# Gate sums moved from the v passes to VectorE beside the products, weights' pieces in one stream through the change of halves, last rows on another queue

## The chip, the cores and the metric

One core of one Trainium2 chip runs the whole program in one launch. The metric is device microseconds of that core; lower is better. The program is one long list of instructions for five engines (TensorE or PE, VectorE or DVE, ScalarE or ACT, GpSimd or POOL, SyncE or SP), each of which works through its own list strictly in order and waits on semaphores. SP does nothing but issue transfers; GpSimd computes and issues some.

## The reference

Input x has 2048 tokens of 1024 values. A is linear attention with 32 heads of 32, B is softmax attention with 32 heads of 32, each with its own qkv weights (1024 by 3072) and output weights (1024 by 1024). A gate mixes them per token:

```python
x = A_x
g = _sigmoid((x * gate_w).sum(-1, keepdims=True))
a = _A_ref(x, A_wqkv, A_wo)
b = _B_ref(x, B_wqkv, B_wo)
return g * a + (1 - g) * b
```

## The kernel before, in words

Every product of two fp32 matrices is done as three matmuls (`three`, from line 148): each operand is split into a high part (a cast on ScalarE, line 293) and a low part (a subtraction on VectorE, line 294), and high-high, high-low and low-high are added up in a PSUM bank of 128 by 512. A 128x512 matmul is the unit.

The work has two parts. The first, up to about 480 us, is written out by hand: for each half J of the tokens (J = 0, 1; 1024 tokens, two column blocks jj) come **v passes** and then **quads**. The second, from there to the end, is a list planned at build time (`linear`, `maxima`, `heads_`, `output`), with a model of each engine's time in `T`.

**v passes** (`v_pass`, line 427, with the loops of both halves that call it). For k = 0 to 7, one 128-row block of x and of B's v weights: x is loaded, split, and 8 banks get 24 matmuls. Raw blocks stay in four raw tiles per pair of k, from which `sides` (four VectorE differences) and `split_sides` make the operands T1, T2 and T3 of a Strassen-like product. At the end the 8 banks are copied by ScalarE to SBUF (`v_out`, line 357) through four buffers, `v_outs`, and stored. After that TensorE can use the banks again.

**Quads** (`quad`, line 475; `quads`, line 631). Eight per half; one quad makes two column blocks of q or k in seven products of 12 matmuls each, on six banks in turn. ScalarE and VectorE combine the products (lines 495 to 514), split the results and SP stores them (`qk<-mid`). After each product (and what is emitted behind it) `next(side)` advances side streams by one **turn**; `beside` advances several. Turns are an order in the program, not a time: an engine gets to what a turn emitted when it has done all before it. The streams are the next quad's weights (`quad_weights`), T4's split (`late_side`), the spill of x to DRAM (`spill_rest`), the gate, and the pieces of B's output weights.

**Ring.** Weights of v passes and quads lie in a ring of 13 pairs of places (`RINGW`), used in turn.

**Gate.** `gate_add` (line 383) runs inside the v passes: for each k and jj ScalarE multiplies a raw x block by the gate weights of its rows (line 388) into a scratch tile of the quads (P1, C11, H11, W2), and GpSimd adds that into `gate_sum` (line 390). During the quads eight one-column matmuls sum over the rows, and ScalarE takes the exponential.

**Pieces** (`wo_parts`, from line 522). B's output weights in 4 row pieces of 7 combinations: ScalarE casts the high part (532), GpSimd subtracts the low part (533), may form the next difference (line 550 and the like) and load the next raw piece (529), and stores both parts to DRAM (537). One pair of buffers serves all pieces, so a cast waits for the stores before. A piece is issued every `PIECE_STEP` = 3 turns, 14 pieces in each half's quads; none in a half's last quad or in the v passes.

**Tail.** When the last softmax head is done (`finish`, `store_part`, line 1300), its 32 rows are copied from SBUF into the output stage's operand tiles (`load_rest`, line 1607, its transfer 1611), four token blocks at a time, by SP. SP's list at this place also holds whole weight tensors of 1 MB (`big<-woS`, `big<-woW`) and the linear branch's rows (`big<-ra`). The output stage's first full product, X21, needs the rows; line 1680 adds a product onto the linear branch's rows.

Of the kernel before, what the change touches and what calls it, by code (L numbers as in the profile page):

```python
# [41 lines left out]
PIECE_STEP = 3  # L42
# [6 lines left out]
def kernel(  # L49
# [73 lines left out]
    big = [None if i in (15, 18, 20) else big_tile(i, F32R) for i in range(NBIG)]  # L123
# [218 lines left out]
    RAW_BIG = (20, 15, 18)  # L342
# [8 lines left out]
    v_outs = [P1, C11, H11, W2]  # L351
# [11 lines left out]
    gate_wt, gate_sum, gate_b = kvb[:, 0, :NK], halves(zrep), bank[6]  # L363

    def gate(J):

        yield
        yield
        for t in range(2 * TPC):
            nc.tensor.matmul(gate_b[:, t:t + 1], gate_sum[t // TPC][:, t % TPC * P:(t % TPC + 1) * P], ones[:, :1],  # L370
                             start=True, stop=True)
        g = g_sb[:, 2 * TPC * J:2 * TPC * (J + 1)]
        nc.scalar.activation(g, gate_b[:, :2 * TPC], AF.Exp, scale=-1.0)
        yield
        if J:
            nc.vector.tensor_scalar_add(g_sb, g_sb, 1.0)
            nc.vector.reciprocal(g_sb, g_sb)
            nc.vector.tensor_scalar(omg_sb, g_sb, -1.0, 1.0, op0=ALU.mult, op1=ALU.add)
            yield

    gate_t = [C11, H11, P1, W2]

    def gate_add(raws, k):

        for jj in range(2):
            acc, raw, w = gate_sum[jj], raws[jj + 2 * (k % 2)], gate_wt[:, k:k + 1]
            to = gate_t[(2 * k + jj) % len(gate_t)] if k else acc
            nc.scalar.activation(to, raw, AF.Copy, scale=w)
            if k:
                nc.gpsimd.tensor_add(acc, acc, to)  # L390
# [57 lines left out]
    def quad_weights(raws, J, f):  # L448
# [7 lines left out]
        part(0, w11)  # L456
        part(6, w22)
# [10 lines left out]
        yield  # L468
# [53 lines left out]
    def wo_parts(i0, i1):  # L522

        z0, z1 = halves(zrep)
        hi_w, lo_w = (big[15][:, i * C:(i + 1) * C] for i in (2, 3))

        def load(z, m, i, **add):
            if i < i1:
# [17 lines left out]
        for _ in range(PIECE_STEP):  # L546
            yield
# [1352 lines left out]
```

## Time and profile before

| | |
|---|---|
| median of 3 runs | 2876.86 us (2874.42 to 2880.17) |
| the profiled execution's own time | 2881.64 us |
| its span, first to last instruction | 2879.9 us |
| TensorE busy | 98% |
| VectorE, GpSimd, ScalarE busy | 82%, 72%, 57% |
| mean granted TensorE clock | 0.990 |
| HBM over the span | 151 GB/s |

Busy shares are means over the whole span; the stages before 480 us and the tail behind 2700 us differ from it. A full stretch of 20 us holds 90 matmuls of 128x512.

### The profile page before, as it was taken

The numbers are of one execution on the slowest core, as the hardware profiler recorded it, in microseconds if no ns is written. First come the engines' busy times: TensorE is split into PE (matmuls) and PEld (weight loads), VectorE is DVE, ScalarE is ACT, GpSimd is POOL, SyncE is SP. The second block draws the span as 40 slices with busy tenths as digits, with TensorE's granted clock in tenths as the row PEclk, the third lists the DMA queues.
The fourth block names the chain that finished last, engine by engine and source line by source line (L and its number), as shares of the span: only waits on it lengthen the run. The fifth ranks groups of instructions, "written<-read, shape, count | busy, mean of one in ns | idle before, by whom it ended". The sixth has DMA issues, their size and how long they took to land.

```text
span 2879.9 us, 46927 instructions
## 1 busy us (share of the span) xinstructions
PE 2815.7 (98%) x15880; PEld 2051.5 (71%) x15880; DVE 2348.8 (82%) x3745; ACT 1649.3 (57%) x3093; POOL 2073.2 (72%) x1078
## 2 busy tenths in 40 slices
PE   8998999999999999999999999999999999999899
PEld 6876777777667766776677767776776667666587
DVE  7877774788888888888888888888878888887678
ACT  5334432176666666666676666666666566656422
POOL 3333234099999999999899999889879988887000
PEclk9999999999999999999999999999999999999999
DMA  7886888633343334343433344455666555545764
GB/s 231 260 260 193 258 272 236 204 96 99 99 123 95 102 105 132 97 105 99 115 104 101 104 116 138 149 170 178 180 189 182 143 155 142 144 119 158 259 198 154
DMA packets 398988, 451.14 MB, mean 157 GB/s; under 512 B 106382, under 2 KB 234638, under 8 KB 396956
## 3 DMA queue, kind: packets, MB, share of 16 engines
q1 hardware_dynamic: 377244, 410.90, 47.1%
q0 software_dynamic: 21504, 37.24, 6.0%
q8 instruction: 127, 2.08, 0.3%
q14 instruction: 113, 0.93, 0.1%
HBM read 305.93 MB, written 127.66 MB: 151 GB/s over the span
## 4 chain that ended last, share of the span: by engine, by line
PE 80%; DMA 3%; DVE 1%; issue 1%; SPq 1%; ACT 0%; POOL 0%; ACTq 0%; DVEq 0%; POOLq 0%
PE bank L1358 16%; PE bank L1216 16%; PE bank L1508 15%; PE bank L152 10%; PE bank L155 10%; PE bank L157 10%; DMA woS<-big 1%; DMA v<-mid 1%; PE bank L1280 1%; SPq L169 1%; PE bank L1006 0%; PE bank L895 0%; DMA xh<-mid 0%; DMA xh<-xs 0%; DVE big L294 0%
## 5 line engine op out<-in xcount | busy, mean ns | idle before, releaser
L1443 POOL TENSOR_TENSOR big<-big,big 128x512 f32<-128x512 f32 (+2 forms) x694 | 1641.7, 2370 | 108.2 <-ACT big L1361 65.3
L1221 DVE TENSOR_REDUCE mx<-bank 128x1 f32<-128x512 f32 x2048 | 1313.5, 683 | 303.3 <-PE bank L1216 299.9
L1361 ACT ACTIVATE big<-bank 128x512 f32<-128x512 f32 x2048 | 1179.8, 602 | 432.9 <-PE bank L1358 368.2
L1358 PE MATMUL bank<-big,big 128*128 128x512 f32 x1888 | 742.1, 394 | 1.7 <-DMA big<-ml 1.2
L1216 PE MATMUL bank<-big,big 128*128 128x512 f32 x1888 | 739.8, 392 | 1.3 <-ACT big L1361 1.3
L152 PE MATMUL bank<-big,big 128*128 128x512 f32 x1576 | 622.2, 395 | 43.6 <-ACT mid L357 17.4
L157 PE MATMUL bank<-big,big 128*128 128x512 f32 x1572 | 618.5, 393 | 4.7 <-DVE big L294 4.6
L155 PE MATMUL bank<-big,big 128*128 128x512 f32 x1576 | 619.2, 393 | 1.6 <-DVE big L294 1.4
L1508 PE MATMUL bank<-big,mid 128*32 128x512 f32 x4096 | 454.2, 593 | 0.0
L1358 PEld LDWEIGHTS bank<-big,big 128*128 128x128 f32 x1888 | 354.3, 188 | 126.8 <-issue 47.8
L1216 PEld LDWEIGHTS bank<-big,big 128*128 128x128 f32 x1888 | 354.9, 188 | 75.2 <-ACT big L1361 2.6
L152 PEld LDWEIGHTS bank<-big,big 128*128 128x128 f32 x1576 | 299.1, 190 | 112.5 <-ACT mid L357 18.2
L157 PEld LDWEIGHTS bank<-big,big 128*128 128x128 f32 x1572 | 297.9, 190 | 72.3 <-DVE big L294 9.0
L155 PEld LDWEIGHTS bank<-big,big 128*128 128x128 f32 x1576 | 299.4, 190 | 65.5 <-DVE big L294 2.9
L1508 PEld LDWEIGHTS bank<-big,mid 128*32 128x32 f32 x4096 | 143.9, 110 | 264.1 <-issue 263.8
L1459 DVE TENSOR_TENSOR bank<-bank,big 128x512 f32<-128x512 f32 x364 | 251.7, 691 | 5.3 <-ACT big L1361 3.0
L294 DVE TENSOR_TENSOR big<-mid,big 128x512 fp32r<-128x512 f32 (+1 forms) x157 | 119.5, 777 | 61.2 <-ACT big L293 61.1
L533 POOL TENSOR_TENSOR big<-zrep,big 128x512 fp32r<-128x512 f32 x28 | 37.2, 1330 | 171.6 <-ACT big L532 94.1
L1439 POOL TENSOR_TENSOR big<-big,big 128x1536 f32<-128x1536 f32 (+1 forms) x31 | 123.3, 3977 | 44.4 <-ACT big L1361 44.2
L293 ACT CAST big<-mid 128x512 fp32r<-128x512 f32 (+1 forms) x157 | 92.5, 616 | 108.0 <-DVE mid L1627 66.7
L152 PE MATMUL bank<-big,xh 128*128 128x512 f32 x376 | 148.5, 395 | 5.4 <-DMA xh<-xs 5.4
L155 PE MATMUL bank<-big,xh 128*128 128x512 f32 x376 | 148.1, 394 | 0.0
(156 smaller groups left out, 2234.5 us busy)
## 6 DMA issues: line engine op xcount, KB each, us to landing
big<-xs SPq DMA_DIRECT2D x288, 256.0 KB
big<-qk SPq DMA_DIRECT2D x690, 64.0 KB
xh<-xs SPq DMA_DIRECT2D x144, 256.0 KB
qk<-mid SPq DMA_DIRECT2D x128, 256.0 KB
big<-oA SPq DMA_DIRECT2D x84, 256.0 KB
xs<-big SPq DMA_DIRECT2D x64, 256.0 KB
oA<-mid SPq DMA_DIRECT2D x64, 256.0 KB
big<-big POOLq DMA_DIRECT2D x50, 256.0 KB, 5.5
```

The lines of the kernel that those rows point to most:

```text
L152: yield nc.tensor.matmul(ps, sh, mh_, start=(kt == 0), stop=False)
L155: yield nc.tensor.matmul(ps, sh, ml_, start=False, stop=(late and last))
L157: yield nc.tensor.matmul(ps, sl, mh_, start=False, stop=last)
L294: eng.tensor_sub(lo, src, f32(hi))
L1216: nc.tensor.matmul(bank[b], q[:, t % TPC * P:(t % TPC + 1) * P], k[:, j * C:(j + 1) * C], start=True, stop=True)
L1221: nc.vector.tensor_reduce(m[:, t, j:j + 1], bank[b], AX.X, ALU.max)
L1358: nc.tensor.matmul(bank[b], k[:, t * P:(t + 1) * P], q_cols(h, j), start=True, stop=True)
L1361: nc.scalar.activation(pr_t[i][:, j * C:(j + 1) * C], bank[b], AF.Exp, scale=SCALE)
L1439: nc.gpsimd.tensor_add(lacc[:, :qp], pr(0)[:, :qp], pr(1)[:, :qp])
L1443: nc.gpsimd.tensor_add(lacc[:, sl], lacc[:, sl], pr(t)[:, sl])
L1459: nc.vector.tensor_add(lacc[:, qp:] if t == NT - 1 else l_b[:, :n], l_b[:, :n], src)
L1508: nc.tensor.matmul(av_b[j * DH:(j + 1) * DH, :], v[:, t, :], pr(t)[:, j * C:(j + 1) * C], start=(t == 0), stop=(t == NT - 1))
```

## The change

- **Gate.** `gate_add` is gone from the v passes. A generator `gate` runs as a side stream of both halves' quads: for each of 4 column blocks and 8 row blocks it loads x once more (SP, 256 KB), two turns later VectorE multiplies by the gate weights and adds to `gate_sum` (one instruction), and one turn later the next load is issued. Behind the eighth, four one-column matmuls and the exponential follow in the next turn. The gate's weights move from `kvb` to `mneg`.
- **Sides.** The four differences of a pair of k are formed in the first half's v passes one pass earlier, where the gate no longer reads the raw tiles.
- **Pieces.** One stream of 28 pieces through both halves: it goes on in each half's last quad, and in the second half's v passes with two turns per k. `PIECE_STEP` is 4.1, counted by a running counter. Both stores of a piece are issued right behind its subtraction, ahead of the next difference and load.
- **Places.** The ring has 12 pairs. Tile 15 keeps raw pieces, gate sum and gate block. `quad_weights` issues its parts in a slightly other division over the turns. The v results' copies get other buffers: six different ones and two of them twice in the first half, in another order of banks.
- **Tail.** The last head's rows are issued by GpSimd.

The diff, cut to its core:

```diff
-PIECE_STEP = 3
+PIECE_STEP = 4.1
...
-    RINGW = [(16, 0), (16, 1), (17, 0), (17, 1), (19, 0), (19, 1), (14, 0), (14, 1), (20, 0), (20, 1), (15, 0),
-             (18, 0), (18, 1)]
+    RINGW = [(18, 0), (18, 1), (19, 0), (19, 1), (14, 0), (14, 1), (20, 0), (20, 1), (17, 0), (17, 1), (16, 0),
+             (16, 1)]
...
-    RAW_BIG = (20, 15, 18)
+    RAW_BIG = (17, 16, 15)
...
-    v_outs = [P1, C11, H11, W2]
+    v_outs = [[P1, C11, H11, *halves(zrep), W2, *halves(zrep)], [P1, C11, W2, H11] * 2]
...
-    def gate_add(raws, k):
-
-        for jj in range(2):
-            acc, raw, w = gate_sum[jj], raws[jj + 2 * (k % 2)], gate_wt[:, k:k + 1]
-            to = gate_t[(2 * k + jj) % len(gate_t)] if k else acc
-            nc.scalar.activation(to, raw, AF.Copy, scale=w)
-            if k:
-                nc.gpsimd.tensor_add(acc, acc, to)
+    z0, z1, gate_sum, gate_x = raw_w0
+    gate_wt = mneg[:, :NK]
+
+    def gate():
+
+        yield
+        for j in range(NJ):
+            for k in range(NK):
+                dma(gate_x, xT[k * P:(k + 1) * P, j * C:(j + 1) * C])
+                yield
+                yield
+                w = gate_wt[:, k:k + 1]
+                if k == 0:
+                    nc.vector.tensor_scalar_mul(gate_sum, gate_x, w)
+                else:
+                    nc.vector.scalar_tensor_tensor(gate_sum, gate_x, w, gate_sum, op0=ALU.mult, op1=ALU.add)
+                yield
+            for i in range(TPC):
+                nc.tensor.matmul(bank[7][:, i:i + 1], gate_sum[:, i * P:(i + 1) * P], ones[:, :1], start=True, stop=True)
+            nc.scalar.activation(g_sb[:, j * TPC:(j + 1) * TPC], bank[7][:, :TPC], AF.Exp, scale=-1.0)
...
         part(0, w11)
+        yield
         part(6, w22)
         nc.vector.tensor_add(w22, w21, w22)
         yield
         nc.vector.tensor_sub(w21, w11, w21)
         part(1, w12)
+        nc.vector.tensor_sub(w11, w22, w11)
         yield
-        nc.vector.tensor_sub(w11, w22, w11)
         part(3, w22)
+        nc.vector.tensor_sub(w12, w12, w11)
         yield
-        nc.vector.tensor_sub(w12, w12, w11)
         part(4, w11)
-        yield
         part(2, w12)
...
-        hi_w, lo_w = (big[15][:, i * C:(i + 1) * C] for i in (2, 3))
+        hi_w, lo_w = (f32r(z) for z in halves(zrep))
+        at, turn = [1.0], count()
...
+        def wait():
+            at[0] += PIECE_STEP
+            while next(turn) + 1 < at[0]:
+                yield
...
         def part(m, i, z):
             nc.scalar.copy(hi_w, z)
             nc.gpsimd.tensor_sub(lo_w, z, f32(hi_w))
-
-        def out(m, i):
             for p, src in enumerate((hi_w, lo_w)):
                 nc.gpsimd.dma_start(wo_d[m][p][:, i * C:(i + 1) * C], f32(src))
-            for _ in range(PIECE_STEP):
-                yield
...
             part("W11", i, z1)
             nc.gpsimd.tensor_sub(z1, z1, z0)
             load(z0, "W22", i, accum_op=ALU.add)
-            yield from out("W11", i)
+            yield from wait()
...
-        gate_add(raw_x0[k // 2], k)
         v_pass(0, k, V_BANKS[0], range(TPC) if k == 0 else None)
-        if k >= 2:
-            i = k // 2 - 1
-            if k % 2:
-                split_sides(raw_x0[i], 0, i)
-            else:
-                sides(raw_x0[i], i)
+        if k % 2:
+            sides(raw_x0[k // 2], k // 2)
+        elif k:
+            split_sides(raw_x0[k // 2 - 1], 0, k // 2 - 1)
...
-    for t in range(2 * TPC):
-        v_out(0, t, bank[V_BANKS[0][t]], v_outs[t % len(v_outs)])
+    for t, to in zip((0, 1, 6, 2, 3, 4, 5, 7), v_outs[0]):
+        v_out(0, t, bank[V_BANKS[0][t]], to)
...
-    quads(0, lambda: load_pair(raw_x1[0], 1, 0), spill_rest(0), gate(0), wo_parts(0, KH // 2))
+    quads(0, lambda: load_pair(raw_x1[0], 1, 0), spill_rest(0), gate_, parts)
     load_pair(raw_x1[1], 1, 1)
-    quad(0, QUADS - 1, change())
+    quad(0, QUADS - 1, beside(change(), parts))
     for k in range(NK):
+        next(parts, None)
         v_pass(1, k, V_BANKS[1])
-        if k < 2:
-            for kk in (2 * k, 2 * k + 1):
-                gate_add(raw_x1[k], kk)
...
+        next(parts, None)
...
-    quads(1, lambda: load_v1(raw_a, range(KH)), spill_rest(1), gate(1), wo_parts(KH // 2, KH))
+    quads(1, lambda: load_v1(raw_a, range(KH)), spill_rest(1), gate_, parts)
+    for _ in gate_:
+        pass
...
-            dma(to[LAST, KH - 1], avs[j * DH:(j + 1) * DH, i * P:(i + 1) * P])
+            nc.gpsimd.dma_start(to[LAST, KH - 1], avs[j * DH:(j + 1) * DH, i * P:(i + 1) * P])
```

More of the change, by code (lines that the diff above doesn't have):

```diff
@@ L671 @@
                 pass
[L672 to L674 removed]
+    for i, b in enumerate((16, 17)):
+        w_t[i] = big[b] = big_tile(b, F32R)
     quad_w = quad_weights(raw_a, 0, 0)
@@ L1772, in output @@
                 load_ra(n + 1)
-    quad(1, QUADS - 1, leave())
+    quad(1, QUADS - 1, beside(leave(), parts))
+    assert next(parts, None) is None
     xh_t[2] = sb.tile([P, 2 * HK * P], F32R, name="xh")
```

67 lines of the change are left out of this document (24 added, 43 removed).

## The prediction

> **What bounds the kernel now.** I read the page first, then the waits of TensorE, then a table by stretches of 20 us, and only then the timelines of the engines.
>
> ```profile
> PE 2815.7 (98%) x15880; PEld 2051.5 (71%) x15880; DVE 2348.8 (82%) x3745; ACT 1649.3 (57%) x3093; POOL 2073.2 (72%) x1078
> ```
>
> TensorE is busy nearly all the time, so a change that leaves the matmuls as they are can win only TensorE's gaps, and the slow clock behind them. The waits of TensorE (total, times, longest) name few and long ones:
>
> ```profile
> PE bank L152 <- ACT mid L357: 17.4, 2, 8.9
> PE bank L152 <- ACT big L293: 12.8, 2, 8.0
> PE bank L152 <- DVE mid L506: 11.1, 2, 6.0
> PE bank L157 <- DVE big L294: 4.6, 6, 1.5
> ```
>
> The table by stretches places them. Columns: busy us (and count) of PE, PEld, DVE, ACT, POOL, then granted clock, DMA share, GB/s.
>
> ```profile
> 20.00:40.00 20.00, 18.48 (x74) 14.36 (x73) 19.83 (x22) 12.40 (x23) 9.83 (x8) 0.91 0.74 250
> 40.00:60.00 20.00, 13.61 (x58) 10.34 (x56) 19.73 (x27) 7.83 (x14) 4.92 (x3) 0.98 0.52 158
> 60.00:80.00 20.00, 16.72 (x76) 14.03 (x77) 10.56 (x18) 11.57 (x23) 1.34 (x2) 0.85 0.85 267
> 80.00:100.00 20.00, 20.00 (x90) 16.57 (x89) 16.65 (x25) 6.62 (x12) 4.94 (x5) 1.00 0.66 199
> 160.00:180.00 20.00, 13.99 (x53) 11.14 (x52) 15.39 (x22) 7.74 (x14) 8.87 (x12) 0.83 0.73 228
> 240.00:260.00 20.00, 14.82 (x60) 11.41 (x59) 14.90 (x14) 10.76 (x19) 11.26 (x8) 0.93 0.46 152
> 260.00:280.00 20.00, 18.48 (x80) 14.98 (x79) 19.65 (x21) 9.18 (x16) 11.63 (x7) 0.98 0.17 44
> 280.00:300.00 20.00, 11.10 (x44) 8.73 (x43) 8.18 (x14) 10.05 (x18) 0.00 (x0) 0.83 0.99 302
> 380.00:400.00 20.00, 14.86 (x65) 12.03 (x64) 13.55 (x18) 6.35 (x12) 7.80 (x9) 0.93 0.90 269
> 400.00:420.00 20.00, 20.00 (x82) 16.38 (x81) 16.04 (x23) 7.95 (x15) 6.61 (x8) 0.90 0.93 283
> ```
>
> A full stretch holds 90 matmuls, one per 0.227 us; what is missing of 90 is the loss, gap and slow clock together. First v passes and the turn into products (20 to 80): 16+32+14 = 62 missing, **14.1 us**. Second v passes (240 to 300): 30+10+46 = 86, **19.5 us**. One wait inside each half's products: 37, **8.4 us**, and 25+8 = 33, **7.5 us**. The tail follows below.
>
> **The change part by part.** Durations are those of the profiled execution, whose own time is 2881.64 us; the runs' median, 2876.86, is 4.8 lower, and the sum is set on the median.
>
> *Gate sums leave the v passes.* GpSimd's additions go (their group, then timelines of GpSimd, VectorE and ScalarE: start, us, what):
>
> ```profile
> L390 POOL TENSOR_TENSOR zrep<-zrep,mid 128x512 f32<-128x512 f32 x28 | 45.7, 1665 | 53.9 <-ACT mid L388 53.9
> 38.42 6.49 POOL L390 TENSOR_TENSOR zrep<-zrep,mid 128x512 f32<-128x512 f32 x4 [6.12 <-ACT mid L388]
> 42.01 3.46 DVE L294 TENSOR_TENSOR big<-mid,big 128x512 fp32r<-128x512 f32 x2
> 48.77 1.28 DVE L294 TENSOR_TENSOR big<-mid,big 128x512 fp32r<-128x512 f32 x2
> 62.65 2.04 ACT L357 COPY mid<-bank 128x512 f32<-128x512 f32 x4
> ```
>
> Beside an addition a VectorE subtraction takes 1.73 us, without it 0.64: some 1.1 us more for each of the 14 additions of a half, 15 us of VectorE. VectorE is full from 20 to 60 (the table), and its late end is what holds ScalarE's copies of the banks at 62.65, for which TensorE waits 8.5 us. With these 15 us gone, and the side differences put one pass earlier, VectorE ends before TensorE. I take 12.6 of the 14.1 us, leaving 1.5 (bounds 9 to 14.1). In the second half the cause begins earlier:
>
> ```profile
> 242.76 0.72 ACT L388 ACTIVATE mid<-xh,kvb 128x512 f32<-128x512 f32 x1 [7.21 <-DMA qk<-mid]
> 290.26 2.04 ACT L357 COPY mid<-bank 128x512 f32<-128x512 f32 x4
> ```
>
> The gate's scaled copy waits 7.2 us for a scratch tile whose store is under way; VectorE stands behind it, then runs slowed, and everything up to the bank copies at 290.26 is late. All of it goes. Five of the weights' pieces come into this stage, each with a GpSimd subtraction or two. I take 17.5 of 19.5 (bounds 10 to 19.5).
>
> *The pieces.* ScalarE's copy of a piece waits for the stores of the piece before (two rows of the waits, then timelines of GpSimd and ScalarE):
>
> ```profile
> ACT big L532 <- DMA woS<-big: 30.6, 12, 4.9
> ACT big L532 <- DMA woW<-big: 24.7, 10, 4.9
> 157.80 1.61 POOL L550 TENSOR_TENSOR zrep<-zrep 128x512 f32<-128x512 f32 x1
> 159.72 0.91 POOL L529 DMA_DIRECT2D zrep<-in_b_wo  x1 [0.31 <-POOL zrep L550]
> 166.15 0.62 ACT L532 CAST big<-zrep 128x512 fp32r<-128x512 f32 x1 [3.88 <-DMA woW<-big]
> ```
>
> That is 55.3 us over 28 pieces, 2.0 each; it is what makes VectorE later from quad to quad until a bank is not free (line 506, 6.0 us). The step itself grows little: the counter also moves in the test that ends a wait, so 4.1 counts are 3.1 turns, 8.5 us at 2.73 a turn (12 matmuls) against 8.2. But now the two stores are issued right behind the subtraction, ahead of the difference and the load: 1.6 + 0.9 us sooner on three pieces of seven, the load alone on three. In the second half's products only six pieces are left, done by turn 18 of 49; the wait there lies in the stretch 380:400, far behind turn 18 of products that begin near 292, and goes in any case. I take both, −15.9 (bounds 0 to −15.9 for this alone).
>
> *The gate beside the products.* 32 loads of 256 KB on SP, 32 VectorE instructions, one set every three turns. Nearest rows (a group; two DMA rows with KB and median us to landing):
>
> ```profile
> L1680 DVE SCALAR_TENSOR_TENSOR big<-mid,omg_sb,big 128x512 f32<-128x512 f32 x24 | 17.9, 747 | 0.2
> zrep<-in_b_wo POOLq DMA_DIRECT2D x12, 256.0 KB, 3.8
> woS<-big POOLq DMA_DIRECT2D x16, 256.0 KB, 6.0
> ```
>
> 24 us of VectorE, 1.8 in 20, lie in its idle time there (4 to 6 of 20 in the product rows). From the load's issue to its use are two turns, 5.5 us: the nearest load lands in 3.8, stores in the same stage take 6.0. Behind the waiting instruction stand VectorE's sums and splits, for which TensorE's banks and weights wait; on SP each load stands behind the qk stores. I take +4 us (bounds 0 to +16, half a microsecond a step).
>
> The four matmuls that end each quarter wait, in TensorE's own order, for the last addition, issued one turn before. How late VectorE is shows in TensorE's and VectorE's timelines, at the first quad and at the fourth, where the first set falls (turn 26, behind the fifth product):
>
> ```profile
> 79.94 0.39 PE L157 MATMUL bank<-big,big 128*128 128x512 f32 x1
> 82.26 0.69 DVE L504 TENSOR_TENSOR mid<-bank,mid 128x512 f32<-128x512 f32 x1
> 137.06 0.39 PE L157 MATMUL bank<-big,big 128*128 128x512 f32 x1
> 142.47 0.68 DVE L504 TENSOR_TENSOR mid<-bank,mid 128x512 f32<-128x512 f32 x1
> ```
>
> In the first quad the fifth product ends at 80.33 and VectorE comes to its sum 1.9 us later; in the fourth it ends at 137.45, VectorE comes at 142.47, and the new addition stands just ahead of that: TensorE would stand 5.0 us. Such waits fall in the first half once, in the second twice (turns 25 and 49); the set that falls on that half's first turn finds its sum ready. A gap of this size costs about 2 us more in clock (6.0 and 8.4 above). So 3 × 7 = +21 (bounds 0 to +27).
>
> The Trainium skill (SBUF — State Buffer, section "SBUF: two separate sides") says a VectorE operation with two SBUF inputs and a GpSimd one lock each other out for a whole instruction. The 1.73 us beside 0.64 agree; by it additions beside a piece's subtraction would wait too, an estimate of up to 8 us of VectorE's time, inside the bounds of the +4.
>
> *Costed at nothing.* A ring of 12 pairs instead of 13: the seventh weight overwrites what the current quad's second product read, and its split is put behind ScalarE's copy of that product's sum, so the wait is over already; uncovered, up to one turn a quad. The other v buffers and weight places: no instruction more.
>
> *The tail.* The last head's rows go from SP to GpSimd (a stretch; timelines; the third row is the chain's own; then a DMA row):
>
> ```profile
> 2710.00:2720.00 10.00, 10.00 (x53) 6.94 (x52) 4.89 (x8) 3.70 (x8) 0.00 (x0) 1.00 1.08 369
> 2719.96 0.29 DVE L1300 TENSOR_TENSOR mid<-mid,bank 128x128 f32<-128x128 f32 x1
> 2723.61 11.68 DMA xh<-mid
> 2730.30 0.88 SPq L169 DMA_DIRECT2D big<-ra  x2
> 2736.03 0.79 PE L152 MATMUL bank<-big,big 128*128 128x512 f32 x1 [7.97 <-ACT big L293]
> big<-qk POOLq DMA_DIRECT2D x30, 64.0 KB, 5.4
> ```
>
> The rows are ready at 2720.25, are issued at 2723.61 behind whole loads of weights (DMA share 1.08 just before) and land at 2735.3. GpSimd is idle and its queue empty: issue near 2721, 5.4 us, split 1.5 more, so 2728 instead of 2736, and TensorE stands no longer there. But the linear branch's rows (big<-ra) stay on SP at 2730.30, behind the same weights, and VectorE needs them before it prepares the fourth product: some 2.5 us come back. I take −5.5 (bounds 0 to −8).
>
> Sum: −12.6 −17.5 −15.9 +4 +21 −5.5 = **−26.5**; 2876.86 − 26.5 = **2850**.
>
> **The rivals.** *The gate's matmuls find their sums ready*, because VectorE is no longer late once the pieces stop holding ScalarE: 18 of the 21 go, 2832. For it: VectorE is only 1.9 us late in a half's first quad, and the pieces' waits come after; against: the additions fill the time that those waits leave, and even 1.9 us is a wait at such a set. Per set 7 becomes 1. *The longer step isn't one*: 3.1 turns still are shorter than the stores' cycle, as the 4.9 us waits suggest, and the first half keeps its 8.4 us: about 2859. *Slower: the gate's loads come late.* A step is 8.2 us: one turn (2.7) from addition to next issue, 0.75 for the addition, the rest for the load. Over 4.7 us of landing VectorE falls behind at each of 32 steps and TensorE follows; (26.5+4)/32 = 0.95 us a step eats the gain, so it decides from 5.7 us on. At the stores' 6.0 the sum is 2850 − 4 + 32 × 1.3 = 2888. Against it: the 3.8 us of the like load. *The tail gives only issue time*: the rows sit among the same engines' backlog, land 11.7 us after 2721, 3 us sooner than now, and the sum is 2853. The Trainium skill (DMA: Bandwidth & Descriptors, section "Issuing engines are not separate DMA queues") says just this; no row of before has a small transfer on the other queue beside such a backlog.
>
> **How the numbers follow.** A difference of 0.2%, 5.8 us, is about what a measurement of this kernel can tell from no change. Chances: forecast 0.41 (2850, own spread ±9), sums ready 0.20 (2832), step no longer 0.15 (2859), loads late 0.09 (2888), tail only issue 0.15 (2853). The range 2826 to 2868 leaves out the late loads and the edges of the others. Slower 0.08, same 0.03 and faster 0.89 come from the same cases.
>
> **What would show it.** After: no group like line 390; VectorE's splits in the v passes at 0.6 to 0.7 us; no TensorE wait on the bank copies over 2 us at the two turns into products; TensorE waits in front of the gate's matmuls of about 5 us, three of them; ScalarE's waits for the pieces' stores clearly under 55 us; the tail's 7.97 us gone with a smaller one behind. The forecast is wrong if VectorE's additions wait for gate_x by microseconds each, if bank waits on line 506 remain, or if the v passes keep a gap for a reason that these rows hide, such as the transfers at 280 to 300 (DMA share 0.99).

## The result, and the profile after

The changed kernel takes 2893.57 us (median; 2892.11 to 2897.14), the kernel before 2876.39 (2874.42 to 2880.17) in runs beside it: **slower**, ratio 1.0060 with a 95% interval of 1.0043 to 1.0077, some 17 us. The forecast was 2850, and the range up to 2868 did not hold the result. Below, a ratio is turned into microseconds at 28.8 us a per cent, since the kernel before moved by some microseconds from one set of runs to the next (2871.4 to 2876.4).

Read the profile after in the same order as the one before. The page's busy shares (TensorE 98%, VectorE 81%, ScalarE 56%, GpSimd 70%) say as little as before. The waits of TensorE (total, times, longest) have new names:

```profile
PE bank L381 <- DVE big L378: 25.3, 3, 9.9
PE bank L152 <- DVE mid L503: 21.3, 6, 7.3
PE bank L152 <- ACT mid L357: 7.5, 1, 7.5
```

Line 381 holds the gate's one-column matmuls, line 378 VectorE's multiply-add for the gate, line 503 a sum of the quads that frees a bank. The bank copies of line 357 stop TensorE once now, and no longer twice. Then the waits of VectorE and of ScalarE, where something is a transfer:

```profile
DVE big L378 <- DMA big<-in_xT: 39.3, 18, 4.4
```

```profile
ACT zrep L534 <- DMA woS<-zrep: 13.3, 5, 5.9
ACT zrep L534 <- DMA woW<-zrep: 9.2, 2, 8.0
```

VectorE waits 39.3 us for the gate's own loads, in 18 of the 32; ScalarE's waits for the stores of the pieces have gone from 55.3 us to 22.5. Of these, 15.1 lie between 229 and 256 us, around the start of the second v passes, where the kernel before issued no pieces. The stretches (same columns as before: busy us and count of PE, PEld, DVE, ACT, POOL, then clock, DMA share, GB/s) show where time was won and lost:

```profile
20.00:40.00 20.00, 20.00 (x90) 16.57 (x89) 19.69 (x33) 11.65 (x21) 1.25 (x2) 1.00 0.97 317
40.00:60.00 20.00, 20.00 (x90) 16.57 (x89) 9.68 (x16) 8.54 (x16) 0.00 (x0) 1.00 0.91 294
60.00:80.00 20.00, 20.00 (x90) 16.57 (x89) 18.23 (x27) 8.38 (x16) 3.07 (x4) 1.00 0.75 218
...
100.00:120.00 20.00, 16.36 (x68) 13.13 (x67) 14.89 (x21) 6.61 (x12) 6.44 (x9) 0.91 0.82 255
120.00:140.00 20.00, 11.17 (x43) 8.79 (x41) 12.70 (x18) 6.18 (x11) 9.48 (x13) 0.76 0.97 310
...
240.00:260.00 20.00, 16.84 (x67) 13.08 (x66) 13.77 (x21) 6.29 (x11) 8.39 (x11) 0.91 1.02 338
260.00:280.00 20.00, 20.00 (x90) 16.57 (x89) 19.33 (x26) 10.01 (x18) 7.66 (x9) 1.00 0.63 199
280.00:300.00 20.00, 12.51 (x52) 10.03 (x51) 8.53 (x12) 8.30 (x15) 7.38 (x9) 0.83 1.06 313
```

From 20 to 80 us TensorE is full: the whole loss of the first v passes is gone. From 100 to 140, in the middle of the first products, 69 of 180 matmuls are missing, 15.7 us in one place, where the kernel before had no such hole. The second half's products have holes of the same kind: from 340 to 400 us 85 of 270 are missing, 19.3 us. The second v passes and their turn (240 to 300) still miss 61, 13.9 us, beside 19.5 before.

How the hole at 120 to 140 comes about stands in three timelines of the same microseconds: SP (the gate load that matters), VectorE, TensorE. Columns: start, duration, engine, line, what, and in brackets the idle time before it with what ended it.

```profile
134.46 0.54 SPq L169 DMA_DIRECT2D big<-in_xT  x1
```

```profile
135.15 0.69 DVE L463 TENSOR_TENSOR extra<-extra,mid 128x512 f32<-128x512 f32 x1
140.27 0.75 DVE L378 SCALAR_TENSOR_TENSOR big<-big,mneg 128x512 f32<-128x512 f32 x1 [4.44 <-DMA big<-in_xT]
140.94 0.68 DVE L501 TENSOR_TENSOR mid<-bank,mid 128x512 f32<-128x512 f32 x1
```

```profile
141.07 1.87 PE L381 MATMUL bank<-ones,big 128*128 128x1 f32 x8 [9.90 <-DVE big L378]
```

The load is issued at 134.46; VectorE has nothing else that it may do from 135.84 on, and stands 4.44 us until the block is there at 140.27, 5.8 us after its issue. Behind the addition in VectorE's list stand the sums of the products (line 501), and behind it in TensorE's list the gate's matmuls, which come 9.90 us late. TensorE's clock is granted at 0.76 in that stretch and 0.82 in the next. The 15 steps from the first to the last load of the half (issued at 61.78 and 219.86) take 158.08 us, 10.5 each; the forecast had 8.2. By the timelines of SP and VectorE, a step is 3.0 us from the end of an addition to the issue of the next load (the forecast had one turn, 2.7), 6.5 from the issue to the next addition (4.7) and 1.0 for the addition itself (0.75). The 18 loads for which VectorE waited took 4.4 to 8.2 us from issue to use, 5.6 in the middle. Some were issued late as well: this one came 5.1 us after the end of the addition before it, and SP had issued a qk store 0.5 us ahead of it.

### The profile page after: what moved, and what is told of

Same layout as the page of the kernel before. It is cut to its first block, busy times and chain, and to the rows that moved or that the text cites. A ratio compares the mean times of both kernels' runs of the same rounds, so it can differ in the third digit from the quotient of the medians.

```text
span 2890.3 us, 46884 instructions
## 1 busy us (share of the span) xinstructions
PE 2819.5 (98%) x15880; PEld 2055.3 (71%) x15880; DVE 2341.8 (81%) x3777; ACT 1630.6 (56%) x3063; POOL 2036.4 (70%) x1066
## 4 chain that ended last, share of the span: by engine, by line
PE 84%; DMA 7%; DVE 5%; issue 2%; ACT 2%; SPq 1%; POOL 0%; ACTq 0%; DVEq 0%
PE bank L1350 16%; PE bank L1208 16%; PE bank L1500 15%; PE bank L152 11%; PE bank L155 11%; PE bank L157 11%; DMA big<-in_xT 2%; DVE big L294 2%; DMA qk<-mid 1%; ACT mid L293 1%; SPq L169 1%; DVE mid L294 1%; DMA xh<-in_b_wqkv 1%; PE bank L1272 1%; DMA v<-mid 1%
## 5 line engine op out<-in xcount | busy, mean ns | idle before, releaser
L152 PE MATMUL bank<-big,big 128*128 128x512 f32 x1576 | 625.2, 397 | 33.9 <-DVE mid L503 21.3
L535 POOL TENSOR_TENSOR zrep<-big,zrep 128x512 fp32r<-128x512 f32 x28 | 40.6, 1449 | 230.3 <-ACT zrep L534 191.7
L293 ACT CAST mid<-mid 128x512 fp32r<-128x512 f32 x64 | 39.7, 620 | 207.9 <-DVE mid L503 103.2
L1431 POOL TENSOR_TENSOR big<-big,big 128x1536 f32<-128x1536 f32 (+1 forms) x31 | 123.2, 3975 | 40.6 <-ACT big L1353 40.4
L294 DVE TENSOR_TENSOR big<-mid,big 128x512 fp32r<-128x512 f32 (+1 forms) x157 | 111.8, 727 | 47.3 <-ACT big L293 47.1
L152 PE MATMUL bank<-big,xh 128*128 128x512 f32 x376 | 147.1, 391 | 0.7 <-DVE mx L1213 0.7
```

The source lines that it names most:

```text
L152: yield nc.tensor.matmul(ps, sh, mh_, start=(kt == 0), stop=False)
L293: nc.scalar.copy(hi, src)
L294: eng.tensor_sub(lo, src, f32(hi))
```

## The experiments

**Theory, from this trace: the gate's loads come late.** Issue and landing together often take longer than the turns they are given, VectorE stops at the addition, all that stands behind it is late, and TensorE's banks with it. **Rivals:** the gate's matmuls in TensorE's own list are the cost, whatever the loads do; the additions cost VectorE's time as such; or the parts of the change that were to win have won nothing. All kernels ran in three rounds beside the kernel before.

**The tail alone.** The kernel before, and only the issuing engine of the last rows changed:

```diff
-            dma(to[LAST, KH - 1], avs[j * DH:(j + 1) * DH, i * P:(i + 1) * P])
+            nc.gpsimd.dma_start(to[LAST, KH - 1], avs[j * DH:(j + 1) * DH, i * P:(i + 1) * P])
```

> The kernel before with one line of the change: the last head's rows are issued by GpSimd instead of SP. Theory of the prediction: the rows no longer stand behind SP's loads, the 7.97 us wait of TensorE goes and 2.5 us come back at the linear branch's rows: 5.5 us faster, 2871. In the trace of the changed kernel the tail's loss against the 0.227 us pitch was 4.1 us instead of 12.4, so 8 us is possible: 2868. Rival (only the issue is saved, the rows share the engines' backlog): 3 us, 2873, with a wait of about 5 us left before X21.

Measured: 2865.65 against 2872.29, ratio 0.9976 (0.9967 to 0.9986), some 7 us faster. In its timeline of TensorE, X21 now waits 1.19 us in place of 7.97; its DMA rows give the landing:

```profile
2724.20 0.50 PE L152 MATMUL bank<-big,big 128*128 128x512 f32 x1 [1.19 <-ACT big L293]
```

```profile
xh<-mid POOLq DMA_DIRECT2D x4, 16.0 KB, 6.1
```

The rows land 6.1 us after the start of their issue, where the chain of the kernel before had 11.68. The issue itself is most of the difference: SP's instruction for the first rows in the kernel before, and GpSimd's here (start, duration):

```profile
2723.61 5.17 SPq L169 DMA_DIRECT2D xh<-mid  x1
```

```profile
2715.88 0.57 POOL L1611 DMA_DIRECT2D xh<-mid  x1 [65.50 <-ACT mid L1671]
```

Counted from the end of the issue, SP's rows land in 6.5 us (11.68 − 5.17), so on SP they lose 4.6 us in the issue and, since the rows are ready at 2720.25, 3.4 us ahead of it; GpSimd issues 0.7 us after its rows are ready (2715.20). The Trainium skill (DMA: Bandwidth & Descriptors, section "Issuing engines are not separate DMA queues") says that another issuing engine saves only the time that the sequencer takes to initiate a DMA, usually small beside the DMA itself. The trace agrees with the first half; the saved time is not small here, 5.17 us beside 6.5. Why SP's instruction took so long (its 15 others of this kind took 0.58 to 1.25 us) no run here shows.

VectorE's wait for the linear branch's rows, which the kernel before did not have, is new:

```profile
2732.27 0.75 DVE L1680 SCALAR_TENSOR_TENSOR big<-mid,omg_sb,big 128x512 f32<-128x512 f32 x1 [3.48 <-DMA big<-ra]
```

TensorE stands 1.15 us behind it.

**The change without the gate.** `gate` does nothing, and both factors are set to 0.5; all else is as changed.

```diff
     def gate():
...
-                    nc.vector.scalar_tensor_tensor(gate_sum, gate_x, w, gate_sum, op0=ALU.mult, op1=ALU.add)
...
+        nc.vector.memset(g_sb, 0.5)
+        nc.vector.memset(omg_sb, 0.5)
```

> The changed kernel without any gate work: no loads of x for it, no additions, no matmuls; the gate is set to one half, so this part of the computation is left out. Theory: the gate beside the products is what made the change slower, and all other edits gain. Then the first part up to the linear stage gets back V pass gains of both halves and the pieces' waits: 2876 - 12.6 - 17.5 - 15.9 - 8 = about 2822. Rival (the pieces in one stream, or the transfers of the products' stage, hold the stage by themselves): above 2850, with waits on line 503 of over 5 us left.

Measured: 2823.32, ratio 0.9828 (0.9811 to 0.9844): 49.5 us faster than before, and all but the same as the 51.5 that the forecast's other terms add up to. That is partly luck: the pieces gave more than their term and the second v passes less, as the table in the next section has it. So the gate costs the changed kernel 1.0060 − 0.9828 = 2.32%, **67 us**; the forecast had +25. The stretches of this kernel (one in the first products, then those from 240 to 300):

```profile
120.00:140.00 20.00, 20.00 (x90) 16.55 (x89) 14.93 (x24) 8.36 (x15) 7.65 (x10) 1.00 1.06 343
...
240.00:260.00 20.00, 8.77 (x38) 6.91 (x37) 13.21 (x20) 8.45 (x16) 4.79 (x7) 0.81 0.93 261
260.00:280.00 20.00, 19.18 (x78) 15.06 (x76) 8.80 (x13) 8.24 (x15) 6.02 (x7) 0.94 0.92 286
280.00:300.00 20.00, 19.45 (x86) 16.12 (x87) 17.13 (x24) 7.76 (x14) 6.69 (x8) 1.00 0.67 204
```

The first products run full, 90 each. But from 240 to 300, 52 + 12 + 4 = 68 matmuls are still missing, 15.4 us, with no gate at all. This kernel comes to the second v passes earlier, so a second count goes by the work: from their first matmul to the first of the products behind them it takes 57.4 us (201.62 to 258.97), the kernel before 62.0 (229.89 to 291.86). By both counts the change wins some 4 us of this stage without its gate, where the forecast had 17.5.

**Which part of the gate costs it.** Three kernels, each the changed one with one part taken out. The first loads only the first block and adds that one 32 times:

```diff
-                dma(gate_x, xT[k * P:(k + 1) * P, j * C:(j + 1) * C])
+                if j == k == 0:
+                    dma(gate_x, xT[k * P:(k + 1) * P, j * C:(j + 1) * C])
```

> The changed kernel with the gate's loads left out but the first one (all 32 additions use the same block of x, so the gate's values are not those of the reference). Theory A (loads come late): VectorE waited 39.3 us for gate_x, 18 times; without, its lateness goes, the waits in front of the gate's matmuls fall from 25.3 us to under 12, those on line 503 from 21.3 to under 8, the second v passes end without the 7.5 us wait: about 2850. Rival B (TensorE waits for the gate's matmuls because of their place in its list, loads or not): matmul waits stay at 20 us or more, 2885. Rival C (the 24 us of additions are the cost): 2885 or more, with line 503 waits unchanged.

Measured: 2857.33, ratio 0.9947 (0.9932 to 0.9962): 32.5 us better than the changed kernel. The waits of TensorE:

```profile
PE bank L382 <- DVE big L379: 15.8, 3, 8.9
PE bank L152 <- DVE mid L504: 5.1, 3, 2.9
```

The bank waits fall from 21.3 us to 5.1, and the gate's matmuls wait 15.8 in place of 25.3. So the loads are the largest part, and 15.8 us of the matmuls' waits are there without them. (This kernel's gate values are not the reference's; its amount of other work is.)

The second keeps the loads and issues each quarter's matmuls two turns later, ahead of the next quarter's first addition:

```diff
+        def total(j):
...
+                    if j:
+                        total(j - 1)
```

> The changed kernel with the four matmuls that end each quarter issued two turns later, ahead of the first multiplication of the next quarter (the last quarter's as before, at the end). Rival B (their place in TensorE's list is the cost): the waits of 9.9 and 6.6 us go, with some 2 us of slow clock each: about 2873. Theory A (VectorE is late because of its waits for the loads; the matmuls only show it): the same lateness returns as waits on banks, line 503, and the time stays within 5 us of the changed kernel, 2889 to 2894.

Measured: 2885.03, ratio 1.0043 (1.0028 to 1.0058), between the two expectations and, by the intervals, not to be told from the changed kernel. The waits of TensorE and VectorE:

```profile
PE bank L152 <- DVE mid L508: 23.6, 7, 7.2
PE bank L370 <- DVE big L385: 17.2, 3, 8.9
```

```profile
DVE big L385 <- DMA big<-in_xT: 41.6, 18, 4.8
```

The two sets that moved and waited before still wait, 5.3 and 3.0 us in place of 9.9 and 6.6; the last set stays where it was and waits 8.9. With the loads late, VectorE is late by more than two turns at these places.

The third does both, so that additions and matmuls are left alone:

> The run without reloads (all additions use one block, the gate's values are not the reference's), with the matmuls two turns later as well. What is left of the gate is 24 us of additions. The run without reloads took 2857, the one without any gate 2823. If TensorE's wait at the matmuls (15.8 us there, and 2 us of clock behind each) is a cost of its own: 2857 - 14 = about 2843. If it only shows how late VectorE is, the lateness returns at the banks (line 503): 2853 to 2857.

Measured: 2845.11, ratio 0.9897 (0.9875 to 0.9919), 14.4 us better than without the loads alone. Its waits of TensorE:

```profile
PE bank L370 <- DVE big L386: 6.2, 2, 3.5
PE bank L152 <- DVE mid L509: 4.6, 3, 2.9
```

What is left to the kernel without a gate, 0.9897 − 0.9828 = 0.69%, 20 us, is the price of additions and matmuls as such. Its stretches show how it is paid:

```profile
120.00:140.00 20.00, 16.52 (x63) 13.28 (x62) 17.41 (x25) 7.76 (x16) 5.86 (x8) 0.83 0.94 299
140.00:160.00 20.00, 20.00 (x90) 16.55 (x89) 17.71 (x26) 7.46 (x15) 7.72 (x9) 1.00 0.93 290
...
320.00:340.00 20.00, 17.12 (x70) 13.77 (x69) 17.50 (x24) 7.38 (x14) 5.94 (x8) 0.91 0.85 275
```

Most stretches of the products are full, with VectorE at 17 to 17.7 of 20: on the average the additions have room. A few are not: 27 matmuls are missing at a set of the gate's matmuls (a wait of 3.5 us), 20 at one bank wait of 2.9 us, and in both the clock is down. The time is lost at single waits of 3 us, each of which costs more than its length (6.1 and 4.5 us of matmuls here), and not spread over the additions. The gate's matmuls themselves are a smaller part: the set in the first of these stretches takes 1.41 us, so the four some 5 to 6 us, an estimate from that one.

**Loads earlier.** All work is kept; each load is issued right behind the addition before it, three turns ahead of its use in place of two:

```diff
-                dma(gate_x, xT[k * P:(k + 1) * P, j * C:(j + 1) * C])
-                yield
...
+                load(j * NK + k + 1)
```

> The changed kernel with each load of the gate issued right behind the addition that frees its buffer, in the same turn, so three turns ahead of its use instead of two; the additions and matmuls stay at their turns. Theory A (loads come late, the mean wait was 2.2 us and the longest 4.4): 2.7 us more of lead take most of it, VectorE's waits for the loads fall from 39.3 us to under 12, and the time falls by some 25 us, to about 2867. Rival (SP's order is the limit: SP now stands for the addition a turn earlier, and the qk stores and the quads' weights queue behind it): waits for the loads shrink but others grow, 2885 or more.

Measured: 2866.95, ratio 0.9970 (0.9960 to 0.9981): 26 of the 32.5 us of the loads come back, and the change as a whole turns from slower to faster. VectorE's wait for the loads:

```profile
DVE big L383 <- DMA big<-in_xT: 11.0, 7, 3.1
```

Seven waits of 11.0 us in place of eighteen of 39.3. The same loads and the same additions, one turn more for the landing: that supports the theory's mechanism. The seven loads that VectorE still waited for took 4.9 to 8.4 us from issue to use, no less than before; what grew is the lead. TensorE's waits for the quads' sums fall from 21.3 us to 6.0 and those of the gate's matmuls from 25.3 to 17.3, while the wait at the second turn into products grows from 7.5 to 11.7. The edit also puts each load ahead of that turn's qk stores in SP's list, and no run tells these two effects apart. The kernel is still 41 us above the one without the gate.

**The pieces alone.** The kernel before, with its step of 3, and the two stores issued right behind the subtraction:

```diff
             nc.gpsimd.tensor_sub(lo_w, z, f32(hi_w))
-
-        def out(m, i):
             for p, src in enumerate((hi_w, lo_w)):
                 nc.gpsimd.dma_start(wo_d[m][p][:, i * C:(i + 1) * C], f32(src))
+
+        def out(m, i):
```

> The kernel before with only the order inside a piece changed: both stores issued right behind the subtraction, ahead of the next difference and the next load. The prediction's term for the pieces: ScalarE's waits for the stores (55.3 us) fall by about half and both waits on line 506 (6.0 and 5.1 us, 15.9 with the clock behind them) go: about 2857 to 2860. Rival: the landing of the stores, not their issue, sets the cycle: 4 us or less, 2868 to 2872.

Measured: 2850.05 against 2875.75, ratio 0.9916 (0.9889 to 0.9943), 24 us faster. ScalarE's only wait for the stores in the list is the first row; two stretches follow that hold 53 and 65 matmuls before, and then one at the start of the linear stage:

```profile
ACT big L532 <- DMA woS<-big: 3.6, 3, 2.0
```

```profile
160.00:180.00 20.00, 20.00 (x90) 16.57 (x89) 17.38 (x24) 7.77 (x14) 6.65 (x8) 1.00 1.00 310
...
380.00:400.00 20.00, 20.00 (x90) 16.57 (x89) 17.43 (x25) 8.73 (x16) 7.95 (x9) 1.00 0.96 306
...
480.00:500.00 20.00, 20.00 (x90) 16.57 (x89) 15.91 (x24) 1.76 (x3) 0.00 (x0) 1.00 0.55 174
```

In the kernel before, the last of these was not full (the stretch, and the wait of TensorE inside it):

```profile
480.00:500.00 20.00, 16.86 (x62) 13.30 (x61) 2.91 (x5) 1.76 (x3) 0.00 (x0) 0.83 0.71 185
```

```profile
490.08 0.79 PE L152 MATMUL bank<-big,xh 128*128 128x512 f32 x1 [3.14 <-DMA xh<-xs]
```

28 matmuls, 6.4 us, were lost there at a wait of 3.14 us for a reload of x and the slow clock behind it, and with the stores issued sooner that is gone too. The order of two lines in one helper does all of it; the longer step is not needed for it. The DMA rows show what else the order does: the loads of the pieces, now issued on GpSimd's queue behind two stores of 256 KB and no longer ahead of them, take 5.6 us to land. The row of all 24 in the kernel before has 3.9 (the forecast's row, of 12 of them, 3.8).

```profile
zrep<-in_b_wo POOLq DMA_DIRECT2D x24, 256.0 KB, 3.9
```

```profile
zrep<-in_b_wo POOLq DMA_DIRECT2D x24, 256.0 KB, 5.6
```

The stores gain what the loads lose: now ahead, they land in 5.3 us (`woS`) and 4.0 (`woW`) in place of 6.0 and 5.2. So the stores are done earlier on two counts: they are issued sooner, and they land sooner.

**The gate in the v passes, summed by VectorE.** The changed kernel, but the sums are formed where the kernel before formed them, from the raw blocks in SBUF (no load), by one VectorE instruction each (no GpSimd addition, no ScalarE copy). The first half's accumulators take the tile that gave the v copies their extra buffers, so those go back to four:

```diff
+    def gate_add(raws, J, k):
...
+            acc, raw = gate_acc[J][jj], raws[jj + 2 * (k % 2)]
...
+                nc.vector.scalar_tensor_tensor(acc, raw, w, acc, op0=ALU.mult, op1=ALU.add)
```

> The changed kernel with the gate's sums back in the v passes, but on VectorE: one multiply-add (0.75 us) per block on the raw tile that is there, into two accumulators, no reload, no scaled copies on ScalarE, no GpSimd additions. Eight matmuls in the third turn of each half's products. Theory: 12 us more VectorE work per half, where VectorE is at its limit late; some of the v passes' gain is lost, the products' stage has no gate: 2823 (no gate at all) + 4 + 10 = about 2837. Rival (VectorE bounds the v passes as in the kernel before): 20 us or more of waits at the two turns into products, 2850 or more.

Measured: 2838.40, ratio 0.9876 (0.9854 to 0.9898): faster than both kernels, with the whole computation done. Its waits of TensorE:

```profile
PE bank L152 <- ACT mid L357: 21.5, 2, 14.2
```

The products are free of the gate; the cost, some 14 us over no gate, is back at the two turns (7.3 us at the first, 14.2 at the second).

**What holds the second turn.** The last four kernels look for the 11 to 14 us that TensorE stands there. In the first, without the gate, the reloads of the v weights are spread over the turns, since VectorE waits there for a scratch tile whose store (`qk<-mid`) is on its way:

```diff
-        load_wv_again(range(NK - 3))
+        load_wv_again([0, 1])
```

> The run without any gate work (the gate is set to one half), with the v weights' reloads spread over the last quad's turns, one k a turn, instead of five ks in the first. Why the second v passes still ended with a wait of 11.2 us without any gate: theory F1, VectorE's T4 difference needs the tile whose qk store stood on SP behind 14 reloads, 7.64 us of wait, and all of the stage runs later by it. Then the wait for the store falls to 3 us or less, the 11.2 to about 6, and the time from 2823 to about 2817. Rival F2: ScalarE's copies of the banks stand behind casts of the quad's weights, whose raw tiles are loaded late whatever VectorE does: 11.2 stays above 9, 2821 to 2825.

Measured: 2822.2, ratio 0.9828 (0.9811 to 0.9844), no change, as rival F2 has it: VectorE's wait for the store goes from 7.6 us to 3.9, TensorE's at the turn from 11.2 to 9.4, and no time is won. What the rival names stands in ScalarE's timelines, ahead of the first bank copy: in the kernel before (copy at 290.26) and in the one without the gate (copy at 257.36).

```profile
280.39 0.62 ACT L293 CAST big<-mid 128x512 fp32r<-128x512 f32 x1 [3.10 <-DMA mid<-in_b_wqkv]
283.98 0.62 ACT L293 CAST big<-xh 128x512 fp32r<-128x512 f32 x1 [2.96 <-DMA xh<-in_b_wqkv]
```

```profile
245.13 0.62 ACT L293 CAST big<-mid 128x512 fp32r<-128x512 f32 x1 [3.06 <-DMA mid<-in_b_wqkv]
249.18 0.62 ACT L293 CAST big<-xh 128x512 fp32r<-128x512 f32 x1 [3.42 <-DMA xh<-in_b_wqkv]
```

Two casts of the next quad's weights wait some 3 us each for their raw blocks, with and without the gate. SP issues these loads only at 277.47 and 242.25, because their tiles hold differences of x until the casts of those are done. Without the gate the issue comes 40.6 us into the stage in place of 47.6, so 7.0 us sooner; from the issue to the first bank copy it takes 15.1 us in place of 12.8, with casts of pieces now among the rest. The difference is the 4.6 us of the count above. No run moved these loads.

In the second, on top of the kernel with VectorE's gate in the v passes, the first bank copies stand ahead of the last casts of the quad's weights in ScalarE's list:

```diff
+    outs = list(zip((2, 3, 4, 5, 6, 7, 0, 1), v_outs[1]))
+    for t, to in outs[:3]:
+        v_out(0, 2 * TPC + t, bank[V_BANKS[1][t]], to)
+    for _ in quad_w:
+        pass
```

> The run with the gate's sums on VectorE in the v passes, and the first copies of the banks (two in the first half, three in the second, in the order in which the products take the banks) ahead of the quad weights' last casts on ScalarE. Theory F2 (the copies stand behind those casts): the waits of 7.3 and 14.2 us at the turns into products fall to under 3 and under 6 us, with about 4 us of slow clock: from 2838 to about 2822. Rival: the first product then waits for its weights instead, the same chain on VectorE, and the gain is 4 us or less, 2834 or more.

Measured: 2833.11, ratio 0.9867 (0.9852 to 0.9882), the fastest of the kernels that compute everything, though the gain of 5 us over the last one is within the intervals. TensorE's wait at the first turn falls from 7.3 us to 2.2, at the second it stays at 14.0. ScalarE's timeline there:

```profile
268.02 0.62 ACT L537 CAST zrep<-big 128x512 fp32r<-128x512 f32 x1 [6.92 <-DMA woW<-zrep]
268.54 1.55 ACT L357 COPY mid<-bank 128x512 f32<-128x512 f32 x3
```

The copies stand behind a piece's cast, which waits 6.92 us for the stores of the piece before. The edit left the two casts that wait for the weights ahead of them as well (3.07 and 3.38 us here). Both edits together:

> Copies first and reloads spread, on the run with the gate's sums on VectorE in the v passes: if both hold, the sum of both, 2822 - 4 = about 2818. If the reloads' order matters only while the copies are late: as with the copies alone, 2821 to 2824.

Measured: 2836.44, ratio 0.9874 (0.9859 to 0.9888): neither expectation holds, and by the intervals it is not to be told from the copies alone. The last one takes away what the timeline names, the pieces issued at the ends of passes 6 and 7 and at the start of 7:

```diff
-        next(parts, None)
+        if k < NK - 1:
+            next(parts, None)
         v_pass(1, k, V_BANKS[1])
...
-        next(parts, None)
+        if k < NK - 2:
+            next(parts, None)
```

> The kernel with the gate summed in the v passes and the first bank copies ahead of the last casts, and no piece of the weights' change issued at the ends of passes 6 and 7 of the second half, nor at the start of pass 7. Theory: in the second half a piece's cast that waits for its stores stands on ScalarE ahead of the first bank copies. Then TensorE's wait at that half's turn into products goes from 14.0 us to about 7, and the time from 2833 to about 2825. Rival: the copies wait for the last quad's own chain, whatever stands ahead of them. Then the wait stays at 13 to 15 us and the time at 2830 or more.

Measured: 2834.75, ratio 0.9870 (0.9852 to 0.9887). The wait is halved, as the theory has it, and the time is the same, as the rival has it. ScalarE's and TensorE's timelines show why:

```profile
275.87 2.43 ACT L357 COPY mid<-bank 128x512 f32<-128x512 f32 x4 [5.60 <-DMA v<-mid]
```

```profile
264.10 0.79 PE L152 MATMUL bank<-big,big 128*128 128x512 f32 x1 [6.44 <-ACT mid L357]
278.36 3.57 PE L383 MATMUL bank<-ones,big 128*128 128x1 f32 x16 [4.40 <-ACT mid L357]
```

The first wait is 6.44: the first copy now follows the cast that waits 3.29 us for the next quad's weights. The later copies wait 5.60 us for their buffers, whose v stores are on their way, and TensorE stands 4.40 more. From 240 to 300 TensorE does 78 + 44 + 78 = 200 matmuls here and 201 in the kernel with the copies first. (From 200 to 240, where both kernels issue the same, it does 155 and 165, so a difference of 2 us between two single executions says little in this stage.) At this turn several transfers end late together (the DMA share is 1.05 and 1.03 from 260 to 280 in these two kernels), and each edit uncovered the next. That transfers as a whole set its length fits all four runs, but no run took transfers away from it: this stays open.

## Why the prediction was wrong, step by step

| step of the sum | forecast, us | measured, us | from |
|---|---|---|---|
| first v passes and turn | −12.6 | −14.1 | stretches 20 to 80 of the changed kernel, all full |
| second v passes and turn | −17.5 | about −4 | without the gate: 15.4 lost, 19.5 before; by the work 57.4 and 62.0 |
| pieces | −15.9 | −24 | the pieces alone |
| additions and loads | +4 | +52 | loads 32.5, additions with the matmuls' own time 20 |
| place of the gate's matmuls | +21 | +14 | without loads, matmuls two turns later |
| tail | −5.5 | −7 | the tail alone |
| sum | −26.5 | +17 | |

The parts were measured one after another, some on the kernel before and some on the changed one, so each price holds with the parts ahead of it removed, and the sum is a check and no proof.

**The step that failed is "I take +4 us" for the additions and loads.** The forecast named the mechanism itself, as the rival "the gate's loads come late", with its threshold (landing of 5.7 us) and its time (2888, measured 2893.6), and gave it 0.09. That 2888 is so near is partly luck, since the other terms of that sum were off both ways. What went wrong was the weight. The loads alone cost 32.5 us, twice the upper bound of 16 for loads and additions together. The forecast set the landing by the nearest load of the same size, 3.8 us, and put the stores' 6.0 beside it as the far end. But the 3.8 belonged to loads that were issued ahead of their piece's stores on their queue. The pieces alone show that the same loads take 5.6 when they stand behind two stores, which is the order that the change itself makes (6.0 in the changed kernel, and also 6.0 and 6.1 in the kernels with one gate load and with no gate, so the gate's loads are not what slows them). Of the gate's 32 loads on SP, 31 are issued next behind a store of qk or x, and so they were like the row of 6.0, not like that of 3.8; that the stores ahead are what slows them on SP is argued from this likeness and from GpSimd's queue, and no run took them away. The 18 that VectorE waited for had 5.6 us from issue to use in the middle, the one at 134.46 took 5.8, and the longest of the first half 8.1, as a piece of the chain of waits has it (start, duration):

```profile
188.07 8.13 DMA big<-in_xT
```

**"24 us of VectorE lie in its idle time there"** held on the average and failed at the edges. With additions and no late loads, most stretches run full; but VectorE comes to a few of its sums some 3 us later, and at the banks and the gate's matmuls that is a gap and a slow clock, with the matmuls' own time 20 us in all. An average of idle time doesn't show these places. The smaller statement in that part held: an addition beside a piece's subtraction took 1.8 us, alone 0.75, and the mean of 28 was 938 ns, so this lock cost 28 × 0.19 = 5 us of VectorE, within the 8 worked out from the Trainium skill (SBUF — State Buffer, section "SBUF: two separate sides").

```profile
L378 DVE SCALAR_TENSOR_TENSOR big<-big,mneg 128x512 f32<-128x512 f32 x28 | 26.2, 938 | 39.3 <-DMA big<-in_xT 39.3
```

**The gate's matmuls** wait at just the three places that the forecast named, by 9.9, 6.6 and 8.8 us in place of 5.0 each; part of that belongs to the loads, since 15.8 of the 25.3 remain without them, 5.3 a place on average, the longest 8.9. The rival "the gate's matmuls find their sums ready" falls with these waits.

**The second v passes** are the second step that failed: "All of it goes". The forecast put all that is late up to the bank copies down to the gate's scaled copy and the slowed VectorE. Without the gate the issue of the next quad's weights does come 7 us sooner, but behind it and ahead of the copies stand two waits of ScalarE, 3.10 and 2.96 us, for these raw weights, which the forecast did not look at and which are there without the gate (3.06 and 3.42). So TensorE still waits 11.2 us at this turn with no gate in the kernel. A piece's cast and the v stores were seen to hold the bank copies there too, and taking the cast away did not shorten the stage. The forecast's last sentence named the transfers at 280 to 300 as a thing that could make it wrong, and gave them no term.

**The pieces**: the mechanism was right, ScalarE's copies waiting for the stores, and so was the cause, the stores' earlier issue; the size was too small by the 6.4 us at the start of the linear stage, where the forecast did not look. The rival "the longer step isn't one" falls with its premise, since a step of 3 is enough.

**The tail**: right, and a little small. X21's wait falls to 1.19 us in the changed kernel as well. What was to come back did, as VectorE's wait for the linear branch's rows (3.48 us in the tail alone, 2.12 in the changed kernel), but TensorE loses only 1.15 us of it in the tail alone. The rival "the tail gives only issue time" falls with its number, 3 us, though not with its reason: it kept all of the 11.7 us for the landing, and 5.17 of these were SP's issue.

## What to carry to other kernels

Price a new transfer by a row that stands behind the same kind of work on its queue, not by one of the same size; and look whether the change itself moves that row's place. An instruction that waits for a transfer delays everything behind it on its engine, so issue the transfer as early as its buffer allows: one turn more was worth 26 us here. Where a change bundles edits, price each alone: two lines in another order and the last rows on an idle queue gave 24 and 7 us on the kernel before, beside the 49 that the change gains without its gate, and with the gate summed from blocks already in SBUF the whole is 1.2% faster than before.

## What was not expected of the hardware

- Loads of 256 KB landed in 3.9 us (median of 24) ahead of two stores on GpSimd's queue, and in 5.6 behind them, with nothing else changed in the kernel; the stores went from 6.0 and 5.2 us to 5.3 and 4.0.
- A transfer of 16 KB inside SBUF landed 11.68 us after the start of its issue from SP, behind weights that SP had issued before it, and 5.17 of these were SP's issuing instruction. From GpSimd, with 0.57 us of issue, such transfers landed in 6.1.
- Around the gaps of 9.9 and 7.5 us the granted clock was 0.76 to 0.83 in stretches of 20 us, so a gap in TensorE costs more than its length.
